# Two transformer layers on one core: a part of the attention's value products in three 16-bit groups instead of float32

## The chip, the core and the metric

The kernel runs on one core of a Trainium2 chip. Its engines, as the profile names them, are PE (TensorE, matmuls), PEld (TensorE's weight loads), DVE (VectorE), ACT (ScalarE), POOL (GpSimd) and SP (SyncE, which issues the DMAs). Each engine works through its own instructions in the order in which the program lists them, and waits on semaphores for the others. The metric is the device time of one execution in microseconds (us).

## The reference

The input x has 2048 rows of 512. Two rounds of an attention layer and a dense layer follow, each with a layer norm ahead and a residual behind:

```python
q = (x @ wq).reshape(B, S, H, Dh)          # 32 heads of 16
k = x @ wk;  v = x @ wv                    # one key and value head for all
scores = einsum("bhqd,bkd->bhqk", q, k) * Dh ** -0.5
p = softmax(scores);  o = einsum("bhqk,bkd->bhqd", p, v)
...                                        # o @ wo
h = einsum("bsd,df->bsf", x, w1)           # 512 to 1792
h = maximum(h, 0);  h @ w2
...
x = x + A(layernorm(x));  x = x + B(layernorm(x))
x = x + A(layernorm(x));  x = x + B(layernorm(x))
```

The softmax is taken without the maximum of each row: a bound that is added to the scores keeps the exponentials in range, and a column of ones beside the values gives their sums. A flag tells where a bound was left; then a second, slower program in float32 runs behind the first.

## The kernel before

**Work.** The queries of one layer are cut into 32 units (U; 64 in both layers): a block of 512 rows and four heads. A step (U, kt) takes one unit against 128 keys; there are 1024. `scores` computes half a step: four heads are laid out as two row halves by two parts (`pr`), and per half step eight float16 matmuls of 64 rows by 32 columns (the form that the profile calls 64*32) fill the tile `fst` (128x1024), from which ScalarE writes exp into half of the tile `fp` (128 x 4 x 512, float32; four buffers). `values` multiplies `fp` with `va` (values and ones, 64x32 float32) into two banks, `facc` and `facc2`: eight float32 matmuls, each of them two records in the trace. After a unit's run of steps `keep` adds both banks to the unit's sums (`faccs`) on VectorE or ScalarE, and the banks are free for the next run.

**Dense work.** Everything else of TensorE's (output projection, both dense matmuls, keys, queries of the next rows) is called dense work here. It comes from generators (`self.gens`) in groups of eight 64*32 matmuls; `batch` runs them on two banks, `fmisc`, twelve groups and then twelve more for a pair of jobs as a rule, and VectorE empties the banks. `self.coming` counts the groups left until the next emptying (99 in between). A chain of dense work starts when eight units are done (`follow`, which raises `self.asked`), with a deadline in steps (`CHAINS`).

**Order.** `timed` writes TensorE's order by hand while the program is built. `_Account` keeps a modelled time for each engine; at each turn `choose` looks 24 moves ahead over half steps of scores, value products and dense groups, with prices SCORE 0.216, VALUE 0.858, DENSE 0.2155 and EXP 0.925 us, and takes the way with the least of TensorE's waiting and ScalarE's idling. `made` holds when a step's exponentials can be multiplied; no more than AHEAD = 4 steps are between scores and products. `at(i, fn)` ties other work to a step, such as `make_joins`: it builds four 128x128 matrices on GpSimd with which `joined` sums the last two units at the end.

**Keys.** `keep_keys` copies the values of a key block (4 of 16 key tiles) into `va` and sums the squares of the keys for the bound; `LIFT` is added to every exponent, and the sums must lie between `LMIN` and `LMAX`.

Since a helper records all operations, all instructions carry line 187; the profile is read by tile names (with a leading f).

Of the kernel before, what the change touches and what calls it, by code (L numbers as in the profile page):

```python
# [28 lines left out]
EPS = 1e-5  # L29
LMIN, LMAX = 1e-25, 1e30  # L30
SLACK, LIFT = 1.004, 16.0
UP, ONE, TOP = 256.0, 16384.0, 200.0


SCORE, VALUE, DENSE, EXP = 0.216, 0.858, 0.2155, 0.925
TO_ACT, TO_PE, COPY = 0.2, 0.2, 1.8
FULL, AHEAD, DEPTH, WIDTH, IDLE, DEBT, OVER, LEAST = 30.0, 4, 24, 40, 0.5, 0.04, 11.0, 1.0
LEND, OWED = 3.3, 4.2
# [109 lines left out]
def small(ins):  # L148
    return count(ins[0]) == 64 and cost_of(ins[0]) == 32

# [67 lines left out]
class _Net:  # L218
# [126 lines left out]
    def setup(self):  # L345
# [5 lines left out]
        self.kop = [self.ct(f"kop{i}", [P, S], self.pt) for i in range(2)]  # L351
        self.va = [self.ct(f"va{i}", [P, KT, 32]) for i in range(2)]
        pair = lambda n, shape: (self.ct(n + "h", shape, self.pt), self.ct(n + "l", shape, self.pt))

# [48 lines left out]
    def late_consts(self):  # L403
        nc = self.nc
        nc.gpsimd.memset(self.va[0], self.vs / self.os)
        if not self.exact:
            nc.gpsimd.memset(self.wms, 0.0)
# [183 lines left out]
    def keep_keys(self, L, b, pv):  # L591
        nc = self.nc
        nc.vector.tensor_copy(self.va[L][:, 4 * b:4 * b + 4, 0:DH], pv[:, :, 48:64])
        if not self.exact:
            kk = self.wt("kk", [P, 2, 4, DH], bufs=1)
            nc.vector.tensor_copy(kk[:, 0], pv[:, :, 0:DH])
            nc.vector.tensor_mul(kk[:, 1], kk[:, 0], kk[:, 0])
            nc.vector.reduce_sum(self.ksq[L][:, 4 * b:4 * b + 4], kk[:, 1], axis=AX)
        if self.exact or b + 1 != self.normed[L]:
            self.have[L] += 1  # L600
# [230 lines left out]
    def remaining(self):  # L831

        self.zero_rows([self.kop[1]])
        self.fixed_rows([self.kop[1]])
        self.nc.gpsimd.memset(self.va[1], self.vs / self.os)

    def following(self):
# [149 lines left out]
    def make_joins(self):  # L987

        self.joins = self.ct("joins", [P, 2, 2, P])
        self.nc.gpsimd.memset(self.joins.rearrange("p k u m -> p (k u m)"), 0.0)  # L990
# [269 lines left out]
    def scores(self, U, kt, q, p, pr):  # L1260
# [9 lines left out]
        nc.scalar.activation(p[:, 2 * pr:2 * pr + 2], st, AF.Exp, scale=self.up ** -2)  # L1270

    def values(self, U, kt, p, acc, start, stop):
        for j in range(4):
# [187 lines left out]

    def timed(self, steps, operands, ready, front, back, product, after):

# [3 lines left out]
        first = [self.first(i) for i in range(n)] + [False]  # L1467
        done, made, gate, lag = [], {}, {}, 0.0
        ends = [0.0, 0.0]
        state = (self.now, False, self.sim.at["ACT"], 0.0, 0.0, 0, 0, 0.0, (), 0.0, 0.0)  # L1470

        def moves(st, rate, free, coming):
# [8 lines left out]
            if q:  # L1481
                t = max(now, q[0]) + VALUE
# [3 lines left out]
                yield "product", (t, True, act, ea, eb, k, j + 1, due, rest, waste + t - now - VALUE, idle), free, coming  # L1486
            if (due >= LEAST or step >= limit) and self.gens:
# [32 lines left out]
        while len(done) < n:  # L1520
            k, j, due = state[5:8]
            self.lend(k // 2)
            due = due if self.gens else 0.0
# [11 lines left out]
            if kind == "score":  # L1535
# [3 lines left out]
                else:  # L1539
                    back(step)  # L1540
                    made[step] = max(self.sim.at["ACT"] + 0.1, gate.get(step, 0.0))
                ends = [ends[1], self.sim.at["ACT"]]
                k, cost = k + 1, SCORE
            elif kind == "work":
# [3 lines left out]
                due, cost = due - w, w * DENSE  # L1548
            else:
                product(j)  # L1550
                after(j)
                j, cost = j + 1, VALUE
                done.append(self.now)
# [8 lines left out]
    def run(self):  # L1562
# [85 lines left out]
        def product(i):  # L1648
# [54 lines left out]

        if self.exact:
            self.alternate(n, front, back, product, after, finish_later)
        else:
            self.timed(steps, operands, ready, front, back, product, after)
        if not self.exact:
# [93 lines left out]
```

## Time and profile before

| | us |
|---|---|
| median of 3 runs | 2258.12 (2257.49 to 2260.42) |
| profiled execution, its own time | 2251.75 |
| its span | 2250.0 |
| TensorE busy | 2182.0 (97%) |
| ScalarE busy | 1989.2 (88%) |
| VectorE busy | 735.5 (33%) |
| GpSimd busy | 275.4 (12%) |

A row of a group of instructions reads: engine, operation, output tile <- input tiles, form, shapes and types, x count | busy us, mean ns of one | idle time of the engine ahead of it and who ended it. A row of a window: its bounds, then busy time and count of PE, PEld, DVE, ACT and POOL (of those that occur), TensorE's granted clock, DMA share and GB/s. A row of the timeline: start, length, engine, operation and how many are merged. A row of a tile gives shortest, middle and longest duration in ns, and the first and last start.

### The profile page before, as it was taken

The page shows a single profiled execution, that of the slowest core. Times are in us where ns is not written, and L with a number is a line of the kernel's source. Part 1 is how long each engine was busy: PE and PEld are TensorE (multiplying, and loading weights), DVE is VectorE, ACT ScalarE, POOL GpSimd, SP SyncE. Part 2 cuts the span into 40 slices and gives each one's busy share as a digit, 9 for nine tenths or more (in the row PEclk, how much of TensorE's full clock was granted, in tenths as well). Part 3 has the DMA queues.
Part 4 walks back from the last instruction along what each step waited for, and adds up shares of the span by engine and source line. Part 5 has one row for each costly group of instructions (what it writes and reads, how often), then busy time and mean ns, then how long its engine had stood idle before and what let it go on. Part 6 is the DMA issues. An engine that isn't in the chain of part 4 may idle for free.

```text
span 2250.0 us, 124021 instructions
## 1 busy us (share of the span) xinstructions
PE 2182.0 (97%) x58445; PEld 1292.6 (57%) x58445; DVE 735.5 (33%) x1575; ACT 1989.2 (88%) x2105; POOL 275.4 (12%) x319
## 2 busy tenths in 40 slices
PE   7999999999999999999999999999999999999998
PEld 3444445755667755655557755556755665665643
DVE  7425533223322243222332244332222222222252
ACT  5999999999988999999988789989999999999910
POOL 6217820001100021000110021100000000100000
PEclk9999999999999999999999999999999999999999
DMA  6235623212332142221342154522123211321132
GB/s 155 76 116 183 204 87 99 67 41 52 88 96 68 45 110 59 86 67 40 82 118 71 42 137 151 146 83 66 39 73 117 68 49 60 82 72 55 41 100 72
DMA packets 182545, 194.85 MB, mean 87 GB/s; under 512 B 79312, under 2 KB 115712, under 8 KB 181768
## 3 DMA queue, kind: packets, MB, share of 16 engines
q1 hardware_dynamic: 182024, 186.83, 28.1%
q8 instruction: 458, 7.50, 1.4%
q14 instruction: 63, 0.52, 0.1%
HBM read 120.16 MB, written 51.87 MB: 76 GB/s over the span
## 4 chain that ended last, share of the span: by engine, by line
PE 80%; ACT 14%; DVE 3%; issue 2%; DMA 0%; POOL 0%; SPq 0%; ACTq 0%; DVEq 0%; POOLq 0%
PE facc L187 32%; PE fmisc L187 32%; PE fst L187 17%; ACT fp L187 14%; DVE fxt L187 0%; DVE fbst L187 0%; DVE fkop L187 0%; DVE faccs L187 0%; DVE fqh L187 0%; POOL fbmv L187 0%; DMA fxt<-fxr 0%; DVE fkv L187 0%; DMA flsum<-fod 0%; DVE fqr L187 0%; DVE fxn L187 0%
## 5 line engine op out<-in xcount | busy, mean ns | idle before, releaser
L187 ACT ACTIVATE fp<-fst 128x1024 f32<-128x1024 f32 x2048 | 1960.6, 1029 | 139.0 <-PE fst L187 127.8
L187 PE MATMUL facc<-fp,fva 64*32 64x512 f32 x16384 | 1147.9, 590 | 3.2 <-DVE fseen L187 1.2
L187 PE MATMUL fst<-fqop,fkop 64*32 64x512 f16 x16384 | 972.8, 377 | 36.3 <-ACT fp L187 29.7
L187 PEld LDWEIGHTS <-fkop 64*32 64x32 f16 x16384 | 397.5, 91 | 476.1 <-issue 379.1
L187 PEld LDWEIGHTS facc<-fp,fva 64*32 64x32 f32 x16384 | 379.1, 106 | 122.5 <-issue 32.6
L187 PE MATMUL fmisc<-fw,fhh 64*32 64x512 f16 (+1 forms) x6384 | 315.8, 376 | 3.4 <-DVE fseen L187 2.5
L187 PEld LDWEIGHTS <-fw 64*32 64x32 f16 (+1 forms) x9576 | 224.9, 93 | 115.8 <-issue 43.7
L187 PE MATMUL fmisc<-fxt,fw 64*32 64x512 f16 (+1 forms) x5544 | 245.2, 376 | 3.3 <-issue 1.5
L187 DVE SCALAR_TENSOR_TENSOR fxt<-fmisc,fxt 128x512 f32<-128x512 f32 x156 | 102.6, 684 | 373.3 <-PE fmisc L187 373.3
L187 PE MATMUL fmisc<-fw,fhl 64*32 64x512 f16 (+1 forms) x3192 | 215.9, 376 | 0.0
L187 POOL TENSOR_SCALAR fbmv<-fbmv 128x1 f32<-128x1 f32 x64 | 17.7, 277 | 1576.1 <-DVE fbmv L187 1574.9
L187 PEld LDWEIGHTS <-fhh 64*32 64x32 f16 (+1 forms) x6384 | 150.9, 93 | 87.7 <-issue 39.3
L187 DVE COPY fseen<-fmisc 1x1 f32<-1x1 f32 x266 | 29.6, 142 | 435.1 <-PE fmisc L187 434.9
L187 DVE TENSOR_SCALAR fhh<-fmisc 128x512 f16<-128x512 f32 x98 | 67.2, 686 | 265.7 <-PE fmisc L187 259.0
L187 PE MATMUL fmisc<-fxq,fw 64*32 64x512 f16 x4032 | 153.3, 376 | 0.5 <-issue 0.4
L187 DVE TENSOR_TENSOR faccs<-faccs,facc 128x512 f32<-128x512 f32 x116 | 79.7, 687 | 87.3 <-PE facc L187 78.0
L187 PE MATMUL fmisc<-fwo,fot 64*32 64x512 f16 x2688 | 99.7, 376 | 2.5 <-DVE fseen L187 1.8
L187 PEld LDWEIGHTS <-fhl 64*32 64x32 f16 (+1 forms) x3192 | 78.8, 93 | 31.7 <-issue 8.0
L187 DVE SCALAR_TENSOR_TENSOR fhl<-fmisc,fhh 128x512 f16<-128x512 f32 x112 | 77.5, 692 | 28.2 <-ACT fhh L187 24.8
L187 PEld LDWEIGHTS <-fot 64*32 64x32 f16 (+1 forms) x2736 | 53.1, 93 | 44.5 <-issue 19.5
L187 DVE COPY faccs<-facc 128x512 f32<-128x512 f32 x51 | 35.2, 690 | 122.0 <-PE facc L187 113.9
L187 POOL TENSOR_TENSOR fxp<-fxn,fxp 128x512 f16<-128x512 f32 x56 | 67.4, 1223 | 22.6 <-DVE fxp L187 22.6
(133 smaller groups left out, 941.8 us busy)
## 6 DMA issues: line engine op xcount, KB each, us to landing
fw<-fwd SPq DMA_DIRECT2D x224, 256.0 KB
fod<-faccs SPq DMA_DIRECT2D x62, 256.0 KB
fqop<-fqd SPq DMA_DIRECT2D x152, 98.0 KB
fxt<-in_A_x_dram SPq DMA_DIRECT2D x32, 256.0 KB
fqd<-fqh SPq DMA_DIRECT2D x64, 128.0 KB
foraw<-fod SPq DMA_DIRECT2D x31, 256.0 KB
frinv<-frd SPq DMA_DIRECT2D x31, 256.0 KB
faccs<-in_B_w_dram SPq DMA_DIRECT2D x28, 256.0 KB
```

The lines of the kernel that those rows point to most:

```text
L187: r = fn(*a, **k)
```

## The change

In some steps, about 190 by the change's description, the exponentials are not multiplied as float32. The upper 16 bits of each are read in place as a bfloat16; VectorE writes the float16 remainder (exponential minus upper half) into the lower 16 bits of the same element, half a step at a time (`cut`, two subtractions of 128x1024). The values are kept a second time as a float16 pair, `vp`: 32 columns of upper parts and ones, 16 columns of remainders. `cut_values` then runs three groups of eight 16-bit matmuls: upper halves by upper values, upper halves by the values' remainders (16 columns), remainders by upper values. Both halves of `fp` are read with a pitch of four bytes.

`timed` decides at build time which steps are cut: after a step's second exponential, if a chain has been asked for, dense work is at hand, no other cut is pending, the step is not the next to be multiplied, more than NEAR = 8 dense groups remain in the batch, and VectorE's modelled time is not later than the first exponential's end by more than LATE = 0.3 us. A cut step's product is booked at CUT = 0.648 us, and it may start 0.35 us after the modelled end of its subtractions (HALF = 1.22 us each).

Besides: `LIFT` goes from 16 to 15 and `LMIN` from 1e-25 to 64, so that the remainders fit float16; `make_joins` runs 40 steps before the end instead of at step 160, and its matrices take the space of the query weights `wq2[0]`; `keep_keys` fills `vp`, and GpSimd presets it.

```diff
@@ keep_keys
+            v, vp = self.va[L][:, 4 * b:4 * b + 4, 0:DH], self.vp[L][:, 4 * b:4 * b + 4]
+            nc.vector.tensor_copy(vp[:, :, 0:DH], v)
+            nc.vector.tensor_sub(vp[:, :, 32:48], v, vp[:, :, 0:DH])
@@ make_joins
-        self.joins = self.ct("joins", [P, 2, 2, P])
+        self.joins = self.wq2[0].bitcast(F32).rearrange("p c (u m) -> p (c u) m", u=2)[:, 0:4].rearrange(
+            "p (k u) m -> p k u m", k=2)
@@ new
+    def halves(self, p):
+        n = "p j (q h) -> p j q h"
+        return p.bitcast(F16).rearrange(n, h=2)[..., 0], p.bitcast(BF16).rearrange(n, h=2)[..., 1]
+
+    def cut(self, p, k):
+        low, high = self.halves(p)
+        c = slice(2 * k, 2 * k + 2)
+        self.nc.vector.tensor_sub(low[:, c], p[:, c], high[:, c])
+
+    def cut_values(self, U, kt, p, acc, start, stop):
+        low, high = self.halves(p)
+        vp = self.vp[U // 32]
+        for k, (x, c) in enumerate(((high, slice(0, 32)), (high, slice(32, 48)), (low, slice(0, 32)))):
+            for j in range(4):
+                hf, pr = divmod(j, 2)
+                for i, a in enumerate(acc):
+                    h = slice(64 * i, 64 * i + 64)
+                    self.nc.tensor.matmul(a[32 * j:32 * j + c.stop - c.start], vp[h, kt, c], x[h, 2 * pr + hf],
+                                          start=start and k == 0, stop=stop and k == 2, skip_group_check=True)
@@ timed
+        self.cuts, pend, chance = set(), [], []
+        def value(j):
+            return CUT if j in self.cuts else VALUE
+        def cut_some(last=-1):
+            while pend and (pend[0][1] <= last or max(pend[0][0], self.sim.at["DVE"]) <= self.now + LATE):
+                cut(*pend.pop(0)[1:])
...
+            cut_some()
+            if chance and self.now >= chance[0][0] - LATE:
+                e1, e, i = chance.pop()
+                if (self.asked and self.gens and not pend and i > j and self.coming > NEAR
+                        and self.sim.at["DVE"] <= max(self.now, e1) + LATE):
+                    self.cuts.add(i)
+                    pend += [(e1, i, 0), (e, i, 1)]
+                    cut_some()
+            if pend:
+                i = pend[0][1]
+                made[i] = max(gate.get(i, 0.0), max(max(self.now, self.sim.at["DVE"], pend[0][0])
+                              + len(pend) * HALF, pend[-1][0] + HALF) + 0.35)
...
-                    made[step] = max(self.sim.at["ACT"] + 0.1, gate.get(step, 0.0))
+                    e = self.sim.at["ACT"]
+                    made[step] = max(e + 0.1, gate.get(step, 0.0))
+                    chance[:] = [(ends[1], e, step)]
...
+                cut_some(j)
                 product(j)
                 after(j)
-                j, cost = j + 1, VALUE
+                j, cost = j + 1, value(j)
@@ run
-            at(160, self.make_joins)
+            at(n - 40, self.make_joins)
...
-            self.values(U, kt, ps.pop(i), accs[0], self.first(i), last)
+            (self.cut_values if i in self.cuts else self.values)(U, kt, ps.pop(i), accs[0], self.first(i), last)
```

More of the change, by code (lines that the diff above doesn't have):

```diff
@@ L29 @@
 EPS = 1e-5
-LMIN, LMAX = 1e-25, 1e30
-SLACK, LIFT = 1.004, 16.0
+LMIN, LMAX = 64.0, 1e30
+SLACK, LIFT = 1.004, 15.0
 UP, ONE, TOP = 256.0, 16384.0, 200.0
@@ L36 @@
 TO_ACT, TO_PE, COPY = 0.2, 0.2, 1.8
+CUT, SPLIT = 0.648, 1.6
+LATE, NEAR, HALF = 0.3, 8, 1.22
 FULL, AHEAD, DEPTH, WIDTH, IDLE, DEBT, OVER, LEAST = 30.0, 4, 24, 40, 0.5, 0.04, 11.0, 1.0
@@ L148, in small @@
 def small(ins):
-    return count(ins[0]) == 64 and cost_of(ins[0]) == 32
+    return count(ins[0]) == 64 and cost_of(ins[0]) in (16, 32)
 def duration(eng, op, out, ins):
@@ L352, in setup @@
         self.va = [self.ct(f"va{i}", [P, KT, 32]) for i in range(2)]
+        self.vp = None if self.exact else [self.ct(f"vp{i}", [P, KT, 48], F16) for i in range(2)]
         pair = lambda n, shape: (self.ct(n + "h", shape, self.pt), self.ct(n + "l", shape, self.pt))
@@ L406, in late_consts @@
         if not self.exact:
+            nc.gpsimd.memset(self.vp[0], self.vs / self.os)
             nc.gpsimd.memset(self.wms, 0.0)
@@ L835, in remaining @@
         self.nc.gpsimd.memset(self.va[1], self.vs / self.os)
+        self.nc.gpsimd.memset(self.vp[1], self.vs / self.os)
     def following(self):
@@ L1460, in alternate, with timed @@
                     back(i + 1)
-    def timed(self, steps, operands, ready, front, back, product, after):
+    def timed(self, steps, operands, ready, front, back, product, after, cut):
         n = len(steps)
@@ L1481, in moves @@
             if q:
-                t = max(now, q[0]) + VALUE
+                t = max(now, q[0]) + value(j)
                 rest = q[1:]
@@ L1485, in moves @@
                     rest = (max(rest[0], t + COPY),) + rest[1:]
-                yield "product", (t, True, act, ea, eb, k, j + 1, due, rest, waste + t - now - VALUE, idle), free, coming
+                yield "product", (t, True, act, ea, eb, k, j + 1, due, rest, waste + t - now - value(j), idle), free, coming
             if (due >= LEAST or step >= limit) and self.gens:
@@ L1704, in run @@
         if self.exact:
+            self.cuts = ()
             self.alternate(n, front, back, product, after, finish_later)
         else:
-            self.timed(steps, operands, ready, front, back, product, after)
+            self.timed(steps, operands, ready, front, back, product, after, lambda i, k: self.cut(ps[i], k))
         if not self.exact:
```

## The prediction

> **What bounds the kernel now.** I read the first part of the page, then the chain that ended last, then a table of three stretches, and last the order of time inside one.
>
> ```profile
> span 2250.0 us, 124021 instructions
> ...
> PE 2182.0 (97%) x58445; PEld 1292.6 (57%) x58445; DVE 735.5 (33%) x1575; ACT 1989.2 (88%) x2105; POOL 275.4 (12%) x319
> ...
> PE 80%; ACT 14%; DVE 3%; issue 2%; DMA 0%; POOL 0%; SPq 0%; ACTq 0%; DVEq 0%; POOLq 0%
> ```
>
> TensorE carries four fifths of the chain and ScalarE most of the rest. A busy PE need not be a full one, because the ends of matmuls are modelled; so I count work instead. Starts of successive groups give the price of each kind:
>
> ```profile
> 1000.54 1.06 PE L187 MATMUL facc<-fp,fva 64*32 64x512 f32 x16
> ...
> 1001.39 0.42 PE L187 MATMUL fst<-fqop,fkop 64*32 64x512 f16 x8
> ...
> 1002.04 0.42 PE L187 MATMUL fmisc<-fw,fhl 64*32 64x512 f16 x8
> ...
> 1002.26 0.42 PE L187 MATMUL fst<-fqop,fkop 64*32 64x512 f16 x8
> ```
>
> A step's value products are 16 records (eight float32 matmuls, two records each) and take 1001.39 - 1000.54 = 0.85 us; the kernel's planner says 0.858 and I use that. Eight 16-bit matmuls take 0.216 us (1002.26 - 1002.04 = 0.22; the planner books 0.2155 to 0.216). Now the stretch in which the change can act, after the first dense chain is asked for and before the closing. First all work, then the work on the exponentials' tile alone (columns PE, PEld, DVE, ACT, POOL, clock, DMA share, GB/s):
>
> ```profile
> 340.00:2140.00 1800.00, 1775.69 (x50625) 1095.57 (x50620) 526.37 (x1156) 1666.95 (x1741) 110.53 (x151) 1.00 0.27 77
> ```
> ```profile
> 340.00:2140.00 1800.00, 971.58 (x13856) 327.26 (x13851) 0.00 (x0) 1663.19 (x1732) 0.00 (x0) 1.00 0.27 77
> ```
>
> PE work there: 13856/16 = 866 steps of values at 0.858 = 743 us, and the other 36769 records at 0.216/8 = 993 us; 1736 of 1800 us, 64 us of slack. ScalarE does 1732 exponentials. What one costs at full speed shows in the first of these windows, which ScalarE bounds:
>
> ```profile
> 200.00:250.00 50.00, 46.76 (x1184) 22.06 (x1176) 27.18 (x60) 49.96 (x55) 44.79 (x35) 1.00 0.62 197
> ...
> 450.00:500.00 50.00, 49.94 (x1456) 26.88 (x1455) 9.95 (x23) 48.67 (x52) 0.00 (x0) 1.00 0.12 36
> ...
> 1650.00:1700.00 50.00, 49.38 (x1392) 25.59 (x1383) 13.56 (x34) 49.90 (x54) 8.19 (x12) 1.00 0.28 66
> ...
> 2000.00:2050.00 50.00, 50.00 (x1464) 26.89 (x1456) 10.61 (x26) 47.64 (x51) 0.00 (x0) 1.00 0.20 67
> ```
>
> 49.96/55 = 0.91 us. So 1732 cost 1576 us, and ScalarE has some 220 us of slack in the stretch against PE's 64. The windows 450 and 2000 are full on PE. For 450, this row has the records of its value products:
>
> ```profile
> L187 PE MATMUL facc<-fp,fva 64*32 64x512 f32 x416 | 27.9, 589 | 0.0
> ```
>
> 416/16 x 0.858 + (1456 - 416)/8 x 0.216 = 50.4 us of work in 50 (the window cuts groups at its ends): no slack at all. Window 1650, with 54 activations, is at ScalarE's limit; there a faster PE buys little.
>
> **The change, part by part.**
>
> *The value products of a cut step.* Removed: 16 records, 0.858 us. Added: 24 matmuls in three groups of eight, each streaming 512 columns of 16-bit data. By the rows above a group of eight such takes 0.216 us, so 0.648 us, a gain of 0.210 us. It is not less than 0.648, since each group still streams 512 columns. Two things of these groups the trace does not show: their moving operand takes 16-bit elements four bytes apart, and one group has 16 stationary columns. The dear end for the pitch is the float32 row, whose groups of eight records stream four-byte elements at 0.858/2 = 0.429 us: three of those are 1.287 us, 0.429 more than now. I take 0.648, because the nearest rows in type, columns and tiles are the 16-bit ones, and part of the float32 price must be its passes. For 190 steps: 190 x 0.210 = -39.9 us, at the dear end +81.5 us.
>
> *The subtraction on VectorE*, two of 128x1024 per cut step. The nearest rows also read float32 and a 16-bit tile from SBUF and write float16; the third reads two float32 tiles from SBUF:
>
> ```profile
> L187 DVE TENSOR_TENSOR fot<-foraw,fot 128x512 f16<-128x512 f32 x31 | 21.5, 693 | 1.1
> ...
> L187 DVE TENSOR_TENSOR fot<-foraw,fot 128x256 f16<-128x256 f32 x2 | 0.9, 426 | 1.0 <-ACT fot L187 1.0
> ```
> ```profile
> L187 DVE TENSOR_TENSOR foraw<-foraw,frinv x31: 681/691/1650, 173.9 to 2102.7; 128x512 f32<-128x512 f32 x31
> ```
>
> 256 elements more cost 267 ns, so 1024 elements take 693 + 2 x 267 = 1227 ns; the planner books 1.22. Two per step, 190 steps: 466 us. VectorE goes from 526 to 992 us of the 1800, from 29% to 55%. The cheap end is the 512-element row's 0.69 us, which would only shorten a wait; the dear end is 1.23 + (1.65 - 0.69) = 2.19 us, by the longest of the third row. Behind it on VectorE's queue stand the evacuations of the dense banks (fmisc), the two adds that free the value banks, and the layer norms; PE waits for all three. What covers it: a step is cut only with more than eight dense groups left in the batch. The stretch holds (36769 - 13848)/8 = 2865 dense groups in 866 steps, 3.3 per step of 2.08 us (13848 are the score records of fst there; row below). Eight groups are thus about 5 us, twice the 2.45 us of both subtractions, and PE's cut products are placed 0.35 us after the modelled end. With that cover gone each hit would hold PE for up to 1.23 us.
>
> ```profile
> 340.00:2140.00 1800.00, 831.09 (x13848) 0.00 (x0) 1663.19 (x1732) 1.00 0.27 77
> ```
>
> Of the Trainium skill the rule that speaks most against this part is in SBUF — State Buffer, "SBUF: two separate sides": a VectorE instruction with two SBUF inputs and a GpSimd one that reads SBUF exclude each other for a whole instruction. The trace agrees (691 ns in the middle, 1650 at most). GpSimd is busy 110.53 of 1800 us, 6%; by the rule about 380 x 0.06 = 23 subtractions would be held by up to 0.96 us, 22 us of VectorE time, of which PE would see a small part, since batches without GpSimd work are where most cuts fit.
>
> PE's present waits for VectorE in the long stretch, the two largest of evacuations:
>
> ```profile
> PEld facc L187 <- DVE faccs L187: 3.6, 6, 1.0
> ...
> PE fmisc L187 <- DVE fseen L187: 2.1, 2, 1.8
> ```
>
> VectorE becomes 1.9 times as busy; were these 5.7 us to grow in step, 5 us would be added. Because of the eight-group guard I take 4 us; the ends are nothing and 190 x 0.21 = 40 us, the second a rival below.
>
> *Buffers.* A cut step keeps its exponentials up to 2 x 1.22 + 0.35 = 2.8 us longer. Four buffers cover four steps, 8.3 us; I cost this at nothing. Without that cover the scores, and ScalarE behind them, would wait up to these 2.8 us per cut.
>
> *Value operands in halves, and their memsets.* Per key block one copy and one subtraction of 128x64 more on VectorE, eight times; two memsets more on GpSimd.
>
> ```profile
> L187 DVE TENSOR_TENSOR fkk<-fkk 128x64 f32<-128x64 f32 x8 | 2.7, 344 | 0.3
> ...
> L187 DVE COPY fva<-fmisc 128x64 f32<-128x64 f32 x8 | 1.8, 220 | 0.0
> ```
>
> That is 0.22 + 0.34 = 0.56 us each, 4.5 us in all. Seven of the eight lie under PE work; the first is in the prologue ahead of the key bound's row, where nothing runs beside it: +0.6 us. The memsets (0.5 us each by the 128x512 memset in the rows of the joining matrices below) lie beside loads.
>
> *The joining matrices* move from step 160 to step 984 and into the query weights' space: one memset and four copies on GpSimd, no DMA.
>
> ```profile
> L187 PE MATMUL fmisc<-fxt,fwqh x656: 372/376/634, 17.2 to 1420.4; 64*32 64x512 f16 x160, 128*128 128x512 f16 x4
> ```
> ```profile
> L187 PE MATMUL facc<-faccs,fjoins x8: 592/592/592, 2145.5 to 2148.5; 128*128 128x512 f32 x8
> L187 POOL COPY fjoins<-fident x4: 236/237/238, 347.1 to 347.7; 128x64 f32<-128x64 f32 x4
> L187 POOL MEMSET fjoins<- x1: 517/517/517, 346.6 to 346.6; 128x512 f32 x1
> ```
>
> The weights are last read at 1420 us, the matrices first at 2145, and GpSimd does nothing in the window 2000 above: 0.517 + 4 x 0.237 = 1.5 us hidden by idle time. Uncovered, the closing would start 1.5 us later.
>
> *How much of the 39.9 us arrives.* A cut in a stretch that ScalarE or a latency bounds gives nothing. PE's slack is 64/1800 = 3.6% of the time, but batches in waiting make cuts easy there, and faster PE work pushes further windows towards ScalarE's 0.91 us: 5.3 cuts per 50 us save 1.1 us, and window 450 has 50 - 52 x 0.91 = 2.7 us of it left. I choose 15% lost, 6 us; 4% is the least that the slack suggests, a half the most I can argue.
>
> Sum: -39.9 + 6.0 + 4.0 + 0.6 = -29.3 us. The profiled execution took 2251.75 us, 1.75 around its span; so 2222.5. The median of the three runs, 2258.12, lies 6.4 above the profiled one, and I carry that over: **2229 us**, 1.3% faster.
>
> **The rivals.**
>
> *ScalarE or the planner's pacing takes half.* For it: window 450 already holds 52 activations, 95% of what ScalarE can do, and dense work is paced by steps. Against: 220 us of slack. Half of 39.9 lost and the 4.6 us of delays paid: -15 us, 2243.
>
> *VectorE becomes the wait.* If a subtraction takes over 1.22 + 0.35/2, about 1.4 us, PE stands at the cut products; at 0.2 us of waiting per cut the gain is gone, 2258. For it: the blocked 1650 ns. Against: 691 ns as its middle.
>
> *The pitch costs double* (slower): three groups at 0.429 us, in all 190 steps, from the price of 0.286 us per group on: +81.5 + 4.6 us, about 2344. For it: no 16-bit moving operand in the trace has a four-byte pitch. Against: nothing but the 16-bit rows' likeness.
>
> *The 16-column group changes the array's form* (slower). Between the 64*32 form and another, PE loses time:
>
> ```profile
> 1337.63 0.43 PE L187 MATMUL fst<-fqop,fkop 64*32 64x512 f16 x8
> 1337.99 0.66 PE L187 MATMUL fmisc<-fident,fkv 128*128 128x128 f32 x4
> 1338.58 0.41 PE L187 MATMUL fst<-fqop,fkop 64*32 64x512 f16 x8
> ```
>
> Of the 0.95 us, 0.216 are the scores and about as much the four transposes (4 x 128 columns), so two changes cost some 0.52 us. In each cut: 190 x (0.52 - 0.21) = +59 us, and 4.6: 2322. Against: 16 columns fit a 32-column tile. The skill's TensorEngine Tiling, "Key Properties", states that changing the tiling mode drains TensorE; the rows above agree that a change of form costs, and no run shows which form 16 columns take.
>
> **How the numbers follow.** Forecast 0.70, half of it 0.11, VectorE 0.06, pitch 0.07, form 0.04, and 0.02 for a slowdown I don't name. The forecast's own range is 2215 to 2242 (all but 4% of the 39.9 us arrives and nothing is delayed, -38 us and some 5 us for the plan's luck; 40% lost). The range 2212 to 2262 takes in the first three cases and leaves out the slower ones, 0.13, and some 0.04 below. This kernel's measurement tells 0.2%, 4.5 us, from no change: faster 0.70 + 0.11 = 0.81, same 0.06, slower 0.13.
>
> **What would show it.** Cut products of 24 records whose successors start 0.65 us later (1.29: pitch; about 1.2 with gaps around eight of them: form); subtractions of 1.23 us; waits of PE for VectorE's subtraction under 5 us in all; window 450 with over 52 exponentials; VectorE near 1000 us in the long stretch. Wrong it is if PE's slack in that stretch grows by over 15 us, or if the count of cuts is far from 190.

## The result and the profile after

The changed kernel's median is 2246.6 us (six runs, 2243.15 to 2251.59), that of before in the same rounds 2258.31: a ratio of 0.9946, 95% interval [0.9931, 0.9961], or 12 us faster. Of the 29 us forecast less than half arrived; the direction was right.

The first lines of the page of the kernel after, its chain of waits by engine, and one group:

```profile
span 2247.6 us, 127404 instructions
...
PE 2162.8 (96%) x59949; PEld 1266.5 (56%) x59949; DVE 1231.6 (55%) x1961; ACT 1980.6 (88%) x2111; POOL 279.3 (12%) x321
...
PE 78%; ACT 11%; DVE 5%; issue 2%; DMA 2%; POOL 1%; SPq 0%; DVEq 0%; ACTq 0%; POOLq 0%
...
L189 DVE TENSOR_TENSOR fp<-fp 128x1024 f16<-128x1024 f32 x376 | 505.8, 1398 | 257.5 <-ACT fp L189 257.0
```

TensorE still carries the chain. 376 subtractions are 188 cut steps, and one takes 1.40 us, not the 1.23 of the prediction. The cut products of the same kernel, grouped by form:

```profile
L189 PE MATMUL facc<-fp,fvp 64*32 64x512 f16 x1504 | 91.8, 387 | 0.0
L189 PE MATMUL facc<-fp,fvp 64*32 64x512 bf16 x1504 | 91.5, 387 | 1.7 <-issue 1.7
...
L189 PE MATMUL facc<-fp,fvp 64*16 64x512 bf16 x1504 | 90.8, 386 | 0.0
```

All three groups look alike, the one of 16 columns too. In the order of time, a cut product and what follows it:

```profile
850.06 0.88 PE L189 MATMUL facc<-fp,fvp 64*32 64x512 bf16 x24
...
850.73 0.42 PE L189 MATMUL fst<-fqop,fkop 64*32 64x512 f16 x8
```

The successor starts 0.67 us later; over all undisturbed cut products of the trace the middle spacing is 0.683 us. The windows that the prediction showed, now of the kernel after (columns as before), and the long stretch last:

```profile
200.00:250.00 50.00, 46.41 (x1168) 22.45 (x1175) 33.54 (x70) 49.94 (x55) 43.14 (x33) 1.00 0.61 195
450.00:500.00 50.00, 49.99 (x1536) 28.34 (x1521) 26.09 (x39) 49.08 (x53) 0.00 (x0) 1.00 0.14 45
1650.00:1700.00 50.00, 49.97 (x1448) 30.71 (x1433) 19.36 (x40) 49.28 (x53) 8.17 (x12) 1.00 0.33 85
2000.00:2050.00 50.00, 48.58 (x1456) 27.49 (x1448) 25.17 (x38) 46.51 (x50) 0.00 (x0) 1.00 0.22 68
340.00:2140.00 1800.00, 1761.92 (x52310) 1071.01 (x52295) 1020.28 (x1536) 1664.63 (x1754) 112.90 (x151) 1.00 0.27 78
```

And the long stretch's work on the exponentials' tile alone:

```profile
340.00:2140.00 1800.00, 930.73 (x15424) 245.29 (x10928) 503.14 (x374) 1657.45 (x1738) 0.00 (x0) 1.00 0.27 78
```

VectorE is busy 1020 us, and window 450 holds 53 activations, both as forecast. TensorE's slack did not stay: 374/2 = 187 cuts at 0.683 are 127.7 us; (15424 - 187 x 24)/16 = 683.5 plain products at 0.858 are 586.4; (52310 - 15424)/8 other groups at 0.216 are 995.9. That is 1710.0 us of work in 1800, 90 us of slack where there were 64. Its idle time alone went from 24.3 (1800 - 1775.69) to 38.1 us. Waits of TensorE in this stretch, before (us in total, times, longest):

```profile
PE fst L187 <- ACT fp L187: 12.2, 32, 1.0
PE fmisc L187 <- issue: 2.7, 4, 0.8
...
PE fst L187 <- issue: 1.9, 2, 1.4
```

and after:

```profile
PE fst L189 <- ACT fp L189: 19.1, 42, 1.2
PE fmisc L189 <- issue: 5.6, 10, 1.3
PE fst L189 <- issue: 2.8, 4, 1.2
PE facc L189 <- issue: 2.8, 4, 1.7
PE fmisc L189 <- DVE fqr L189: 1.7, 4, 1.2
PE fmisc L189 <- POOL fsq L189: 1.5, 1, 1.5
PE facc L189 <- DVE faccs L189: 0.8, 1, 0.8
PE fmisc L189 <- DVE fseen L189: 0.6, 2, 0.3
```

The wait of scores for a bank that ScalarE still reads grew by 6.9 us, waits without a named cause by some 6; those for VectorE did not (4.3 us in all before, 4.0 after).

A window of fixed times doesn't hold the same work in both kernels. So I cut each trace at two events instead: the first exponential of step 140 (up to there the order of before and after is the same) and the start of the last matmul of the last value product. Between them lies "the stretch", behind them "the tail". Work counts records with the prices above; slack is the stretch less its work. The first 140 steps end at 304.2 us before and 309.9 after, but at 305.9 in a second profile of the kernel after, and at 310.5 in one without cuts: 5 us of luck. They are the clock's: up to step 140 the trace shows TensorE's granted clock at half for 10.2 us in before and in the second profile of after, for 20.5 us in after and in the kernel without cuts, and 10.2 us more at half speed lose 5.1. This is largely why the two profiled executions (2251.75 and 2249.38) lie closer than the medians. In us, with the timed ratio against the kernel before; each label is explained where its experiment stands:

| kernel | cuts | stretch | work | slack | tail | ratio and interval |
|---|---|---|---|---|---|---|
| before | 0 | 1838.9 | 1771.9 | 67.0 | 106.9 | |
| e4_no_cuts | 0 | 1837.3 | 1771.9 | 65.4 | 106.1 | 0.9997 [0.9982, 1.0011] |
| p1_before_other_plan | 0 | 1844.8 | 1771.9 | 72.9 | 111.2 | 1.0000 [0.9987, 1.0014] |
| after | 188 | 1823.6 | 1736.4 | 87.2 | 114.1 | 0.9946 [0.9931, 0.9961] |
| r_after | 188 | 1819.6 | 1736.4 | 83.1 | 113.3 | 0.9965 [0.9954, 0.9976] |
| p2_after_other_plan | 181 | 1822.4 | 1737.6 | 84.8 | 113.8 | 0.9951 [0.9934, 0.9968] |
| e2_booked_as_measured | 166 | 1826.9 | 1742.9 | 84.0 | 110.0 | 0.9964 [0.9952, 0.9977] |
| e1_no_subtraction | 188 | 1815.6 | 1736.4 | 79.1 | 114.9 | 0.9936 [0.9918, 0.9955] |
| e5_free_plan | 188 | 1813.6 | 1736.4 | 77.1 | 112.8 | 0.9917 [0.9897, 0.9937] |
| e3_in_batch_only | 151 | 1818.6 | 1745.5 | 73.1 | 110.5 | 0.9932 [0.9914, 0.9950] |
| e6_fewer_better | 159 | 1815.2 | 1744.1 | 71.1 | 108.2 | 0.9921 [0.9900, 0.9941] |
| p3_fewer_other_plan | 168 | 1834.7 | 1742.5 | 92.2 | 110.7 | 0.9957 [0.9939, 0.9975] |
| e7_earlier_due | 182 | 1818.2 | 1740.1 | 78.2 | 108.6 | 0.9911 [0.9880, 0.9941] |

Before (mean of the first two rows) to after (mean of its two): work -35.5, slack +19.0, tail +7.2, and 0.8 us in the prologue: about -8.5, beside timed medians of -11.7 and -8.5. So the cuts save what they can, and more than half of it is given back in slack and tail. The experiments ask what that slack is.

### The profile page after: what moved, and what is told of

The parts are those of the page before. It is cut to its first block, busy times and chain, and to the rows that moved or that the text cites. A ratio compares the mean times of both kernels' runs of the same rounds, so it can differ in the third digit from the quotient of the medians.

```text
span 2247.6 us, 127404 instructions
## 1 busy us (share of the span) xinstructions
PE 2162.8 (96%) x59949; PEld 1266.5 (56%) x59949; DVE 1231.6 (55%) x1961; ACT 1980.6 (88%) x2111; POOL 279.3 (12%) x321
## 4 chain that ended last, share of the span: by engine, by line
PE 78%; ACT 11%; DVE 5%; issue 2%; DMA 2%; POOL 1%; SPq 0%; DVEq 0%; ACTq 0%; POOLq 0%
PE fmisc L189 31%; PE facc L189 31%; PE fst L189 16%; ACT fp L189 11%; DVE fbst L189 1%; DMA frd<-flsum 1%; DMA fqop<-fqd 1%; DVE faccs L189 0%; DVE fxt L189 0%; SPq L189 0%; DVE fxn L189 0%; DVE fp L189 0%; DVE fqr L189 0%; DMA frinv<-frd 0%; POOL fbmv L189 0%
## 5 line engine op out<-in xcount | busy, mean ns | idle before, releaser
L189 PE MATMUL fst<-fqop,fkop 64*32 64x512 f16 x16384 | 952.2, 378 | 43.2 <-ACT fp L189 36.5
L189 PE MATMUL facc<-fp,fva 64*32 64x512 f32 x13376 | 937.8, 593 | 3.3 <-issue 2.0
L189 DVE TENSOR_TENSOR fp<-fp 128x1024 f16<-128x1024 f32 x376 | 505.8, 1398 | 257.5 <-ACT fp L189 257.0
L189 PEld LDWEIGHTS <-fkop 64*32 64x32 f16 x16384 | 382.8, 91 | 460.5 <-issue 347.1
L189 PEld LDWEIGHTS facc<-fp,fva 64*32 64x32 f32 x13376 | 296.9, 106 | 100.2 <-issue 26.4
L189 PEld LDWEIGHTS <-fw 64*32 64x32 f16 (+1 forms) x9576 | 201.6, 93 | 132.5 <-issue 41.8
L189 PE MATMUL fmisc<-fw,fhl 64*32 64x512 f16 (+1 forms) x3192 | 202.3, 378 | 0.0
L189 PE MATMUL facc<-fp,fvp 64*32 64x512 f16 (+2 forms) x4512 | 178.2, 386 | 1.7 <-issue 1.7
L189 PEld LDWEIGHTS <-fvp 64*32 64x32 f16 (+1 forms) x4512 | 89.7, 90 | 44.6 <-issue 10.9
```

The lines of the kernel that those rows point to most:

```text
L189: r = fn(*a, **k)
```

## The experiments

The theories in play were: the new operations cost more than booked; the subtractions hold up VectorE's queue and TensorE behind it; TensorE's clock drops more often; the rest of the change costs something; the loss lies in the order that the planner writes, at places where one chain of dense work hands over to the next, and in the closing.

**The prices by themselves** (m1_prices). A kernel of its own, which computes nothing of the reference: eight subtractions of each kind one behind the other, then ten groups of eight matmuls of each kind.

```python
for i in range(8): tensor_sub(wl[:, c], pw[:, c], wh[:, c])   # as in cut(); then other places and types
...
for g in range(10): eight matmuls(v16[:, 0:32], m16)          # flat float16
for g in range(10): eight matmuls(v16[:, 0:32], rh)           # upper halves, pitch of four bytes
for g in range(10): eight matmuls(v16[:, 0:32], mb)           # flat bfloat16
for g in range(10): eight matmuls(v16[:, 32:48], m16)         # 16 columns
```

> This kernel leaves the whole computation out (its output is a copy of x) and runs, eight times each, the VectorE subtraction of 128x1024 in seven layouts, and ten groups each of eight 64*32 matmuls in six layouts. In the changed kernel's trace a subtraction took 1.396 us at the middle (1.341 to 1.803) and not the 1.227 of the prediction, and a cut product 0.683 us and not 0.648. Theory: the four-byte pitch of the 16-bit operands costs both. Then the subtraction into a flat float16 tile takes about 1.23 us and the one in place 1.40, and a group with a pitched moving operand 0.227 us against 0.216 flat; 16 columns or bfloat16 beside float16 change nothing. Rival: the subtraction's 1.40 us is what any float32 minus bfloat16 of this length costs in an idle kernel (all layouts near 1.40), and the 0.683 comes from the change between groups of different kinds (all pure groups at 0.216, only the alternating ones above).

In the order of time, the ten groups of each kind, then groups at the pitch and flat ones by turns, and what follows them:

```profile
29.04 2.35 PE L80 MATMUL a<-m,v 64*32 64x512 f16 x80
31.21 2.44 PE L83 MATMUL a<-pr,v 64*32 64x512 bf16 x80
33.46 2.35 PE L86 MATMUL a<-mb,v 64*32 64x512 bf16 x80
35.62 2.35 PE L89 MATMUL a<-m,v 64*16 64x512 f16 x80
37.78 0.42 PE L92 MATMUL a<-pr,v 64*32 64x512 bf16 x8
38.00 0.40 PE L92 MATMUL a<-m,v 64*32 64x512 f16 x8
...
39.98 8.77 PE L95 MATMUL a<-pr,v 64*32 64x512 f32 x160
```

The starts are 2.17, 2.25, 2.16 and 2.16 us apart. Flat 16-bit data cost 0.216 us a group, the pitch 0.225; neither the type nor 16 columns cost anything. The ten groups by turns take 39.98 - 37.78 = 2.20 us, five of each price, so the change from one kind to the other, the rival, costs nothing either. In the kernel a cut product takes 0.683, not 3 x 0.225 = 0.675; these 0.008 us stay open. The subtractions, by group (place and type of the result, then what is read):

```profile
L53 DVE TENSOR_TENSOR pw<-pr 128x1024 f16<-128x1024 f32 x8 | 12.0, 1498 | 0.0
L51 DVE TENSOR_TENSOR pw<-pw 128x1024 f16<-128x1024 f32 x8 | 11.4, 1430 | 16.4 <-ACT pw L38 16.4
L59 DVE TENSOR_TENSOR pw<-pr,flatb 128x1024 f16<-128x1024 f32 x8 | 11.1, 1387 | 0.0
L57 DVE TENSOR_TENSOR flat<-pr,flatb 128x1024 f16<-128x1024 f32 x8 | 10.8, 1353 | 0.0
L55 DVE TENSOR_TENSOR flat<-pr 128x1024 f16<-128x1024 f32 x8 | 10.7, 1337 | 0.0
L61 DVE TENSOR_TENSOR dst<-pr,q 128x1024 f32<-128x1024 f32 x8 | 10.1, 1259 | 0.1
L63 DVE TENSOR_TENSOR dst<-pr,flatb 128x1024 f32<-128x1024 f32 x8 | 9.8, 1222 | 0.2
```

With a float32 result the old estimate of 1.23 us holds (1222, 1259 ns). A flat float16 result takes 1337 to 1353, whether the halves are read with a pitch or flat; writing it at the pitch takes 1387 to 1498, up to 0.16 us more. So neither theory holds for the subtraction as a whole: the larger part of 1.40 - 1.23 comes with the 16-bit result at this size, the rest with writing at a pitch.

**Cuts without their subtraction** (e1_no_subtraction). The remainders are not formed; the third group multiplies the upper halves again, so the output lacks the remainders. Order and booked times stay.

```diff
-        self.nc.vector.tensor_sub(low[:, c], p[:, c], high[:, c])
+        ins = [p[:, c], high[:, c]]
+        self.sim.run("DVE", low[:, c], ins, duration("DVE", "tensor_sub", low[:, c], ins))
...
-        for k, (x, c) in enumerate(((high, slice(0, 32)), (high, slice(32, 48)), (low, slice(0, 32)))):
+        for k, (x, c) in enumerate(((high, slice(0, 32)), (high, slice(32, 48)), (high, slice(0, 32)))):
```

> The changed kernel with its order of work unchanged, but without the 376 subtractions: the third group of a cut product multiplies the upper halves once more, so the remainders are left out of the result (and the products are wrong by that). VectorE is as free as before the change; TensorE does all of its new work. After step 140 the changed kernel's profile shows 27 us more of TensorE time outside of its work than the one before. Theory A (delays behind VectorE, which takes 1.40 us where the plan books 1.22): most of it comes back, ratio to the kernel before about 0.986 (2227 us), TensorE's time outside work after step 140 back to about 70 us. Theory B (ScalarE or the pacing of dense work takes the gain): nothing comes back, ratio 0.994 to 0.995 (2245 us).

2237.97 us, ratio 0.9936 [0.9918, 0.9955]: close to theory B, far from A. Slack falls by 6.1 us against the two profiles of after, to 79.1, and stays 12.9 above that without cuts. So 500 us of subtractions on VectorE cost about 6 us (1.7 of them a spell of TensorE's clock at half, as shown below), and most of the loss is there without them. So is the wait of scores for ScalarE's banks, read as above:

```profile
PE fst L189 <- ACT fp L189: 18.9, 41, 1.2
```

**Nothing cut** (e4_no_cuts). All else of the change stays: the second copy of the values, the moved joins, the shifted bound.

```diff
-                if (self.asked and self.gens and not pend and i > j and self.coming > NEAR
+                if (False and self.gens and not pend and i > j and self.coming > NEAR
```

> The changed kernel in which no step is ever cut; the split values, the later joining matrices, LIFT and LMIN stay. Theory A and B: as the kernel before within 0.1% (the prologue's 0.8 us), ratio 0.9995 to 1.001. Theory C (the missing gain went into more spells at half of TensorE's clock in the prologue and the closing, which the changed kernel's profile shows at 46 to 54, 66 to 74 and 2152 to 2164 us against 44 to 50 and 2160 to 2166 before, because the later start moves them): some 5 to 10 us slower than before, ratio 1.002 to 1.004.

0.9997 [0.9982, 1.0011]. The rest of the change costs nothing that can be measured.

**Booked as measured** (e2_booked_as_measured). The planner gets the measured prices; its plan then holds 166 cuts.

```diff
-CUT, SPLIT = 0.648, 1.6
-LATE, NEAR, HALF = 0.3, 8, 1.22
+CUT, SPLIT = 0.683, 1.6
+LATE, NEAR, HALF = 0.3, 8, 1.40
...
+        if ins[1].space != bass.MemoryType.PSUM and ins[1].ap[-1][0] == 2:
+            c = n / 2255.0
...
+        if ins and ins[-1].dtype == BF16 and n == 1024:
+            return 1.40
```

> The changed kernel with its plan told the measured prices: the subtraction booked at 1.40 us instead of 1.217, the cut product at 0.683 us instead of 0.648. The plan then cuts 166 steps and not 188 and places products later. Theory A: the gain stays or grows although a ninth of the cuts is gone, ratio 0.991 to 0.995, and TensorE waits less for late subtractions and evacuations. Theory B: the gain falls with the cuts, 166/188 of 0.0054, ratio 0.9952.

0.9964 [0.9952, 0.9977], a little worse than either theory, and slack 84.0: the same as after. That the planner's prices were too low is not what the gain went into.

**The change again** (r_after). The file of after, unaltered.

> The changed kernel again, unaltered, beside the next three. If the first result holds: ratio to the kernel before 0.993 to 0.996. Single runs spread by some 5 us either way, with the number of spells at half of TensorE's clock in the prologue and the closing.

0.9965 [0.9954, 0.9976], slack 83.1, tail 113.3: just above the ratio expected; gain and loss recur.

**Products not delayed either** (e5_free_plan). The 188 steps of after's plan are given from the start, no subtraction is booked or run (as in e1 the remainders are left out), and products needn't wait for any.

```diff
+CUTS = {
+         146, 155, 161, 163, 165, 168, 172, 184, 187, 191, 197, 201, 205, 208, 212, 215, 219, 223, 231, 235,
...
-        self.cuts, pend, chance = set(), [], []
+        self.cuts, pend, chance = CUTS, [], []
...
-                if (self.asked and self.gens and not pend and i > j and self.coming > NEAR
+                if (False and self.gens and not pend and i > j and self.coming > NEAR
```

> The same 188 steps as in the changed kernel are cut, without subtractions on VectorE (the third group multiplies the upper halves again, so the remainders are left out of the result), and the plan knows it: nothing is booked on VectorE and a cut product may follow as soon as its exponentials are done. Without its subtractions but in the old order, the changed kernel stood at 0.9936 (2238 us at the middle of its runs), and its stretch after step 140 still had some 10 us more outside TensorE's work than before the change. Theory B1 (these 10 us are ScalarE and the handovers between chains, which a faster TensorE cannot shorten): no better than that, ratio 0.991 to 0.994. Theory B2 (they come from products that the plan puts late for the subtractions' sake): they return, ratio 0.986 to 0.989, and the stretch after step 140 takes about 1805 us instead of 1816.

0.9917 [0.9897, 0.9937]; slack 77.1, 2 us under e1. Even with the subtractions free in every respect, this order of 188 cuts leaves 11 us more slack than none, which neither VectorE nor the delayed products explain.

**Cuts only inside a batch** (e3_in_batch_only). Between two emptyings of dense banks `coming` is 99; there nothing is cut now.

```diff
-                if (self.asked and self.gens and not pend and i > j and self.coming > NEAR
+                if (self.asked and self.gens and not pend and i > j and 90 > self.coming > NEAR
```

> The changed kernel, but no step is cut between two batches of dense work (the counter of groups left must be under 90 as well as over 8), where layer norms and evacuations use VectorE. The plan then cuts 151 steps. Theory A (subtractions in the handovers delay the chains): the 37 cuts lost cost 37 x 0.175 = 6.5 us of TensorE work and give back at least as much, ratio 0.993 to 0.995, with less TensorE time outside of work. Theory B: the gain falls with the cuts, ratio 0.9955 to 0.997.

0.9932 [0.9914, 0.9950] with 151 cuts. Work is 9.1 us more (2.6 of it 96 dense matmuls that after leaves for the tail), slack 12 us less than in the mean of after and r_after (3.4 of it such spells, which e3 does not have): 37 cuts fewer, and not slower.

**Fewer, with measured prices and no lateness** (e6_fewer_better).

```diff
-CUT, SPLIT = 0.648, 1.6
-LATE, NEAR, HALF = 0.3, 8, 1.22
+CUT, SPLIT = 0.683, 1.6
+LATE, NEAR, HALF = 0.0, 7, 1.4
...
+        if ins[1].space != bass.MemoryType.PSUM and ins[1].ap[-1][0] == 2:
+            c = n / 2255.0
...
+        if ins and ins[-1].dtype == BF16 and n == 1024:
+            return 1.40
```

> A version that might beat both: subtraction and cut product booked as measured (1.40 and 0.683 us), a cut only where VectorE is free when the first exponential ends (LATE 0 instead of 0.3 us), more than 7 groups left instead of 8. The plan cuts 159 steps. Theory A: fewer delays behind VectorE, ratio 0.990 to 0.994. Theory B: 159/188 of the gain, 0.9955.

2236.51 us, 0.9921 [0.9900, 0.9941], with 159 cuts and a slack of 71.1. That looked like a better rule.

**Three orders redrawn** (p1, p2, p3). The same edit in before, after and e6: the planner books an exponential at 0.93 instead of 0.925 us, which changes no work and draws another order.

```diff
-SCORE, VALUE, DENSE, EXP = 0.216, 0.858, 0.2155, 0.925
+SCORE, VALUE, DENSE, EXP = 0.216, 0.858, 0.2155, 0.93
```

> The kernel before with one price of its plan moved by half a per cent (an exponential booked at 0.93 us instead of 0.925), so that the order falls a little differently. Theory E (TensorE's work alone sets the time of the kernel before, so its order hardly matters): ratio 0.999 to 1.001. If the order's luck matters as much here as it may with cuts: 5 us or more either way.

> The changed kernel with the same price moved (0.93 us); its plan cuts 181 steps instead of 188. Theory E (with cuts the gain hangs on how the order falls at the handovers, some 5 to 10 us either way): the ratio leaves the changed kernel's 0.9946 to 0.9965 by 0.002 or more. Rival (the lost gain is a fixed cost of cutting): 0.9945 to 0.997 again.

> The version with measured prices, LATE 0 and more than 7 groups (159 cuts, 0.9921) with the same price moved; its plan cuts 168 steps. If measured prices and free VectorE are what helped: 0.990 to 0.994 again. If it was the order's luck: 0.994 to 0.998.

Before stays (1.0000 [0.9987, 1.0014]), though its slack is 72.9 here; after stays (0.9951 [0.9934, 0.9968]), where theory E expected it to move; e6 falls back to 0.9957 [0.9939, 0.9975], its slack from 71.1 to 92.2. The intervals of e6 and p3 just touch. So e6's gain did not outlast another order under the same rule: between two orders of nearly the same cuts (159 and 168) lie 21 us of slack in the profiles and, by the ratios, 0.0036 or 8 us of time. Beside p1's 72.9 without any cut, the slack of e6 and of e3 (73.1) is not clearly more than that of an uncut kernel. By the same token the advantage of e3 can't be credited to its rule with one order of it run.

**A chain due earlier** (e7_earlier_due). In after, e1, r_after, e5 and p2 the stretch holds 23281 matmuls of dense work, in before 23377: 96 are left for the tail. One chain's deadline is moved by eight steps:

```diff
-CHAINS = (((397, 266), (447, 394), (385, 522), (459, 624)), ((385, 780), (384, 908), (408, 1034), (384, 1152)))
+CHAINS = (((397, 266), (447, 394), (385, 522), (459, 624)), ((385, 780), (384, 908), (408, 1026), (384, 1152)))
```

> The changed kernel with the due step of the last dense chain but one at 1026 instead of 1034 (1024 is the last step). In the changed kernel 96 matmuls more than before the change are left when the last value product starts, and from there to the end it takes 113 to 114 us instead of 106 to 107. Theory D (part of the gain is given back in the closing, because the plan lets that chain run over): the closing falls to 107 to 110 us and the ratio to the kernel before is 0.992 to 0.994; the changed kernel stood at 0.9946 and 0.9965. Rival (the closing's length is the clock's spells, not the work left): closing unchanged at 113 us, ratio as the changed kernel's.

2235.89 us, 0.9911 [0.9880, 0.9941]. The tail as one window, before:

```profile
2143.06:2249.96 106.90, 94.73 (x523) 42.94 (x507) 42.01 (x73) 12.18 (x21) 3.57 (x8) 0.97 0.27 90
```

after:

```profile
2133.52:2247.62 114.10, 99.25 (x619) 44.96 (x603) 42.63 (x75) 12.18 (x21) 3.57 (x8) 0.94 0.23 75
```

and e7:

```profile
2124.61:2233.23 108.62, 94.74 (x523) 42.87 (x507) 41.17 (x72) 12.18 (x21) 3.57 (x8) 0.96 0.28 89
```

619 matmuls against 523: the 96 are back before the tail, and it is 5.1 us shorter than the mean of after's two. That they fell behind the last value product was due to the order of after's plan; e2, e3, e6 and p3, with 151 to 168 cuts, do not have it. The clock acts on the tail too, but does not explain this: while TensorE still works there, it stands at half for 3.4 us in r_after, p2, e6 and e7 alike, and the tails are 113.3 and 113.8 us with the 96 matmuls, 108.2 and 108.6 without. Part of the tail's growth need not be the cuts' at all: p1, without a cut but with 6.8 us at half, has 111.2. The other part of e7's gain is 7 us less slack, again with a new order; what of that belongs to the deadline isn't shown. e7 is the fastest kernel measured here; its interval overlaps those of e1, e3, e5 and e6, by a little those of p2, p3 and of after's first measurement.

**One handover looked at.** Around step 270 dense work passes from projections of the keys on to the next chain. In the order of time, VectorE before:

```profile
570.30 0.69 DVE L187 COPY fkv<-fmisc 128x512 f32<-128x512 f32 x1 [8.27 <-PE fmisc L187]
```

and after:

```profile
569.94 2.65 DVE L189 TENSOR_TENSOR fp<-fp 128x1024 f16<-128x1024 f32 x2 [6.26 <-ACT fp L189]
572.48 0.69 DVE L189 COPY fkv<-fmisc 128x512 f32<-128x512 f32 x1
```

Before, VectorE had stood idle for 8.27 us and takes the bank at once. After, two subtractions lie ahead of the copy. What comes behind is the add that frees the value banks, and TensorE stands for it, in after:

```profile
578.99 1.10 PE L189 MATMUL facc<-fp,fva 64*32 64x512 f32 x7 [0.82 <-DVE faccs L189]
```

and in e1, the same place without the subtractions:

```profile
572.65 0.66 PE L189 MATMUL facc<-fp,fva 64*32 64x512 f32 x7 [0.32 <-DVE faccs L189]
```

Here the subtractions cost 0.50 us. In after TensorE's granted clock then falls (windows of after, the last three numbers being granted clock, DMA share and GB/s):

```profile
574.00:578.00 4.00, 2.65 (x45) 0.88 (x30) 3.84 (x6) 4.00 (x6) 1.59 (x1) 1.00 0.89 325
578.00:582.00 4.00, 3.18 (x46) 1.60 (x53) 1.97 (x8) 1.22 (x2) 0.00 (x0) 0.61 0.20 74
```

and in e1 it does not:

```profile
572.00:576.00 4.00, 3.68 (x96) 1.96 (x103) 1.64 (x8) 2.80 (x3) 0.00 (x0) 1.00 0.30 104
```

Added up over windows of 4 us, such a spell costs 1.7 us of full speed. Between 340 and 2140 us after, r_after, p2, e2, e5 and e7 have two of them, e1, e4, p1 and p3 one, before, e3 and e6 none: 3.4 us in after against 0.9 in the mean of before and e4, so about 2.6 of the 19 us. e3 has the same stall here (0.83 us) without a spell, so a stall alone doesn't decide it. The Trainium skill's TensorE: Matmul & The Clock Gate, "What's actually happening", has a free-running window of about 3.4 us, of which one idle halves the clock. The trace agrees with the half speed and the length (1.7 us lost at half are 3.4), and e3 fits a window that runs freely; but here TensorE was busy 2.65 of the 4 us ahead of it, with no pause named above 0.84 us, so it need not be idle for a whole window.

The mean granted clock is known for every timed execution. It was 0.9939 and 0.9949 in before beside e2 and r_after, 0.9939 beside p2; 0.9920 in e2, 0.9926 in r_after and in p2, 0.9917 in after's own six. As (1 - clock) times the span, that is 11.4 to 13.7 us in before and 16.5 to 18.7 in the four with cuts. So over the whole execution the clock took 3 to 5 us of the gain of e2, r_after and p2, at most, since half speed costs nothing while TensorE waits anyway. It does not do so in every kernel with cuts: e1 and e7 have 0.9937, where the kernel before has 0.9939 beside both. So of the 8 to 9 us by which e1's median lies below those of after and r_after, some 2 to 5 are the clock's. Nor does it make the difference of e6 and p3: 0.9938 and 0.9932 are 13.8 and 15.3 us, 1.5 of their 8.

**All pauses of the dense work.** The same account can be made for each pause in the stretch, from the start of one matmul into `fmisc` to the start of the next. The six pauses over 8 us, the long handovers, hold 12.7 and 14.2 us of slack in before and e4, and 14.7 in after and in r_after. The pauses of 4 to 8 us are ten and eight there, twenty and twenty-two here, and hold 8.2 and 7.4 us there, 13.7 and 14.1 here. The rest of the growth, some 11 us, lies outside these pauses. So the long handovers lost next to nothing, against the theory; the loss is spread over many short waits.

## Why the prediction was right in direction and wrong in size

**The gain of a cut** (190 x 0.210 = -39.9). The count was right, 188. The step "I take 0.648, because the nearest rows in type, columns and tiles are the 16-bit ones" failed by its size: the pitch costs 4% of a group, 0.683 us a step in the kernel, which takes back 188 x 0.035 = 6.6 us. The true value lay between the two ends, near the one I chose. The Trainium skill has a rule for this in Advanced Engine Details and Errata, "SBUF Cachelines": at least two hits on a 16-byte line are needed to absorb the memory's latency, and further accesses to the same line run at full performance. A four-byte pitch gives four hits; read so, the group would cost 0.216, and 0.225 was measured, so here the measurement decides.

**How much arrives** (+6.0 where ScalarE or a latency bounds, +4.0 behind VectorE). This term failed most: slack grew by 19.0, not by 10, beyond the 15 at which the prediction called itself wrong (in its own window of fixed times, from 64 to 90). Of its parts, the subtractions on VectorE's queue were about right: 6 us by e1, of which 1.7 belong to a spell of the clock, against 4 booked. They don't show as waits of the cut products, whose start the plan puts late enough even at 1.40 us; they show in what stands behind them on VectorE, as at step 270. TensorE's wait for banks that ScalarE reads grew by 6.9 us, near the 6.0 booked. It comes with the cuts, in every order that was run: 11.3 to 12.8 us between 340 and 2140 in the three kernels without cuts, 14.1 to 19.1 in all with cuts, and 18.9 in e1. What was not in the sum is the rest, about 6 us: other short waits in an order that the cuts redrew, and the clock's spells. The 12.9 us that stay without subtractions are shown, and about half of them is that wait for ScalarE; that the others are due to the order is shown only so far as another order moved slack by 21 us with cuts (e6, p3) and by some 7 without (p1 against before and e4). How much 188 cuts must lose in the best order remains open; the smallest slack seen with cuts is e6's, 71.1 with 159 of them, against 65.4 to 72.9 without.

**The closing** was not in the sum. 96 dense matmuls slid behind the last value product: the tail grew by 7.2 us, 2.6 of them (96/8 x 0.216) work that the stretch no longer had. e7 shows that about 5 of the 7.2 us could be had back.

**Costed at nothing, rightly:** joins, memsets, the shifted bound, buffers (e4; and no wait for a buffer of the exponentials appears among the rows above). The prologue cost 0.8 us by the first exponential (31.7 before, 32.5 after), 0.6 booked; but single profiles of the same prologue have it between 31.8 (e5) and 33.6 (e4), so this term is not resolved.

**The subtraction** at 1.227 was extrapolated from rows of 512 and 256 elements, which hold for a float32 result of 1024 but not for a float16 one. It cost little, since most of it is covered. The prediction also had GpSimd hold up 23 subtractions for 22 us of VectorE's time. In after five of the 376 took over 1.45 us, the longest 1.80, some 1.7 us more than the middle in all; the seven that overlap work of GpSimd take 1.63 us in the mean, the others 1.39.

**The rivals.** VectorE did not become the wait, although 1.40 us is just the point named: the plan starts the cut products late enough, and none of the waits shown is theirs. ScalarE's share of the loss was the 15%, not the half: window 1650, then at ScalarE's limit, is now TensorE's as well (49.97 of 50, ScalarE 49.28). The result lies near that rival's 2243 for other reasons. Doubled pitch and changed form did not occur. In numbers: -39.5 + 6.6 + 19.0 + 4.6 + 0.8 = -8.5 in the profiles (4.6 is the tail less its moved work), where I had -39.9 + 10.0 + 0.6 = -29.3.

## What to carry to other kernels

A saving per operation, multiplied by its count, is an upper end where an order written out ahead keeps the engine 97% busy: book what the redrawn order loses in short waits and in its last stage, and look at the last stage first: the 5 us of tail that one deadline gave back were worth about as much as all that the subtractions cost. Compare the granted clock of the executions too: here it may have taken 3 to 5 us, where 9 to 12 were gained. Before a rule of the planner is believed, draw the order again with a price that changes no work; here that alone moved a kernel of nearly the same cuts by 8 us. Price an operation that the trace lacks by a row of its own result type and pitch, not by element count alone.

## What was not expected of the hardware

- A 128x1024 VectorE subtraction takes 1222 to 1259 ns with a float32 result, 1337 to 1353 with a flat float16 one, and 1387 to 1498 with one written at a pitch of four bytes.
- A moving operand of 16-bit elements four bytes apart costs 0.225 us per group of eight, 4% more than flat. Stationary operands of 16 columns in the 64*32 form, and bfloat16 beside float16, cost nothing, and neither do groups at the pitch and flat ones by turns.
- TensorE's granted clock halves for about 3.4 us in the middle of a stretch where it is busy most of the time, in some orders twice, in others never. In two profiles of the same kernel (after) step 140 begins its exponentials at 309.9 and 305.9 us, with 20.5 and 10.2 us at half clock before it.
